# SwiGLU feed-forward on one core: half of the first x rows transposed by the DMA crossbar instead of TensorE

## The chip, the core and the metric

The kernel runs on one core of a Trainium2 chip. A core has a matrix engine (TensorE, PE in the profile), a vector engine (VectorE, DVE), a scalar engine (ScalarE, ACT), GpSimd (POOL) and a sync engine (SyncE, SP). SP and ACT also issue DMA transfers; each has a queue of its own (q1 is SP's, q10 ACT's in this profile), and both queues feed the core's 16 DMA engines. The metric is the device time of one execution in microseconds (us); lower is better.

## The reference

```python
# x (1, 2048, 640), w_gate and w_up (640, 1536), w_down (1536, 640), all bf16
def reference(x, w_gate, w_up, w_down):
    g = silu(x @ w_gate)
    u = x @ w_up
    return (g * u) @ w_down
```

## The kernel before

With P = 128 the 640 columns of x are KD = 5 slices and the 1536 hidden columns are KF = 12 "f chunks". The 2048 rows are worked in four blocks of 512 rows (`sb`), each of four 128-row chunks.

**Layouts.** TensorE contracts over the partition axis, so the gate and up products need x transposed: `xT` holds it as [128 of d, 5, 2048 rows]. Block 0 is loaded plainly into `x_sb` (`load_x`, L84) and transposed by TensorE against an identity matrix (L183), five 128x128 transposes per chunk into a PSUM tile `pt`, which VectorE or ScalarE copies into `xT` (L188). Blocks 1 to 3 come transposed straight from memory by the DMA crossbar (`turn_x`, L125, one DMA of 512 rows each on SP's queue).

**A block.** For each f chunk, `proj` (L192) makes five matmuls for the gate (`pg`) and five for the up product (`pu`), each 128 weights columns by 512 rows of x. ScalarE applies Silu (`sg`, L212) and VectorE multiplies with `pu` into `aT` (L213). PSUM has four buffers for `pg` and `pu` together. After twelve f chunks come the products with `w_down`: `po_t` (columns 512 to 639, transposed) and `po_a` (columns 0 to 511, per 128 rows), their copies and the output DMAs (L276, L301). The last four rows of x are worked on VectorE instead: `row_dots` multiplies transposed weights (`wgT`, `wuT`, loaded through the crossbar by `turn_w`, L129) with `x_row`, spread through blocks 1 to 3.

**The head.** `head()` writes by hand the order in which TensorE works until the third f chunk of block 0, while the loads arrive. 18 filler matmuls on a tile of ones (`warm`, L174) come first; then the transposes of chunks 0 and 2, two fillers, the transposes of chunk 1, two fillers. Then the gate product of f chunk 0 for chunks 0 and 2 (one strided operand, `outer_chunks`) and for chunk 1, the up product of f chunk 0 and the gate product of f chunk 1 for the first 384 rows, the transposes of chunk 3, the up product of f chunk 1 for 384 rows, and the four products for the last 128 rows. `keep_order` fixes the order in which each engine issues its instructions as written.

**The loads.** SP: x chunk 0, x chunk 1, parts of the f chunk 0 slices of `w_gate` and `w_up`, the f chunk 1 slice of `w_gate`, x chunk 3, the f chunk 1 slice of `w_up`, then the later weight slices (`W_CHUNKS`: chunks 2 and 3, 4 to 7, 8 to 11; `load_w`, L81), `w_down`, the crossbar load of block 1, `x_row` and the crossbar loads of `wgT`. ACT: x chunk 2 and the other parts of the two f chunk 0 slices (L111), and then a first small Silu (L114) that has its function table loaded. Each DMA takes one of eight hardware semaphores in turn; a DMA whose semaphore is still held by an earlier one waits in the issuing engine for that one to land.

Of the kernel before, what the change touches and what calls it, by code (L numbers as in the profile page):

```python
# [10 lines left out]
def _body(  # L11
# [8 lines left out]
    nc = tc.nc  # L20
    P = nc.NUM_PARTITIONS
    f32 = mybir.dt.float32
    bf16 = mybir.dt.bfloat16
# [3 lines left out]
    B, S0, D = x.shape  # L27
# [5 lines left out]
    KD = D // P  # L33
    KF = F // P
    S_BLK = 512
    NSB = S // S_BLK
    SUB = S_BLK // P
    DA = 512
    Q = 32
    N_WARM, N_GAP = 18, 2  # L40
    T = 4
    WT_STEP = 4
    ROW_J = 0
    W_CHUNKS = [(0, 1), (1, 2), (2, 4), (4, 8), (8, 12)]
    assert D % P == 0 and F % P == 0 and S % S_BLK == 0 and D > DA and SUB == 4

    consts = ctx.enter_context(tc.tile_pool(name="consts", bufs=1))
# [4 lines left out]
    )  # L52

    ident = consts.tile([P, P], bf16)
    x_sb = consts.tile([P, SUB, D], bf16)
    xT = consts.tile([P, KD, S], bf16)
    wg_sb = consts.tile([P, KD, F], bf16)
    wu_sb = consts.tile([P, KD, F], bf16)
# [13 lines left out]
    xt_v = x2.rearrange("s (kd p) -> s kd p", p=P)  # L72
    wg_v = w_gate.rearrange("(kd p) f -> p kd f", p=P)
    wu_v = w_up.rearrange("(kd p) f -> p kd f", p=P)
    wd_v = w_down.rearrange("(kf p) d -> p kf d", p=P)

    def wslice(a, b):
        return slice(a * P, b * P)

    def load_w(eng, dst, src, a, b):  # L80
        eng.dma_start(out=dst[:, :, wslice(a, b)], in_=src[:, :, wslice(a, b)])  # L81

    def load_x(eng, c0, c1):
        eng.dma_start(out=x_sb[:, c0:c1, :], in_=x_v[:, c0:c1, :])  # L84
# [18 lines left out]
    silu_first = consts.tile([P, 1], f32)  # L103
    nc.vector.memset(ones[:], 1.0)  # L104

    load_x(nc.sync, 0, 1)
    load_x(nc.scalar, 2, 3)
    load_x(nc.sync, 1, 2)
    for dst, src, k in ((wg_sb, wg_v, 3), (wu_sb, wu_v, 2)):
        for eng, k0, k1 in ((nc.scalar, 0, k), (nc.sync, k, KD)):  # L110
            eng.dma_start(out=dst[:, k0:k1, wslice(0, 1)], in_=src[:, k0:k1, wslice(0, 1)])  # L111
    load_w(nc.sync, wg_sb, wg_v, *W_CHUNKS[1])
    load_x(nc.sync, 3, 4)
    nc.scalar.activation(silu_first[:], ones[:, 0:1], ACT.Silu)  # L114
    load_w(nc.sync, wu_sb, wu_v, *W_CHUNKS[1])
    for a, b in W_CHUNKS[2:]:
        load_w(nc.sync, wg_sb, wg_v, a, b)
        load_w(nc.sync, wu_sb, wu_v, a, b)
# [1 line left out]
    wgt_v = w_gate.rearrange("d (kf p) -> d kf p", p=P)  # L120
    wut_v = w_up.rearrange("d (kf p) -> d kf p", p=P)

    def turn_x(sb):
        s_sl = slice(sb * S_BLK, (sb + 1) * S_BLK)
        nc.sync.dma_start_transpose(out=xT[:, :, s_sl], in_=xt_v[s_sl])  # L125

    def turn_w(dst, src):
        for a in range(0, KF, WT_STEP):
            nc.sync.dma_start_transpose(  # L129
                out=dst[:, a : a + WT_STEP, :], in_=src[:, a : a + WT_STEP, :]  # L130
            )

    turn_x(1)
    nc.sync.dma_start(
        out=x_row[:],
        in_=x2[S - T : S, :].rearrange("t d -> (t d)").partition_broadcast(P),
# [29 lines left out]
    def do_dots(n):  # L166
        for _ in range(n):
            next(dots, None)
# [3 lines left out]
    def warm(n):  # L172
        for _ in range(n):
            nc.tensor.matmul(  # L174
                pw[:, 0:P], lhsT=ones[:], rhs=ones[:], start=True, stop=True
            )

    def transpose_chunk(c, parts):
        c_sl = slice(c * P, (c + 1) * P)
        for copy, tag, k0, k1 in parts:  # L180
            pt = psum.tile([P, k1 - k0, P], bf16, tag=tag, name="pt")
            for kd in range(k0, k1):
                nc.tensor.transpose(  # L183
                    out=pt[:, kd - k0, :],
                    in_=x_sb[:, c, kd * P : (kd + 1) * P],
                    identity=ident[:],
                )
            copy(out=xT[:, k0:k1, c_sl], in_=pt[:])  # L188

    def proj(ps, w_sb, fc, sb, c0, c1, cols=lambda ap: ap):  # L190
        for kd in range(KD):
            nc.tensor.matmul(  # L192
                cols(ps[:, c0:c1]),
                lhsT=w_sb[:, kd, fc * P : (fc + 1) * P],
                rhs=cols(xT[:, kd, sb * S_BLK + c0 : sb * S_BLK + c1]),
                start=(kd == 0),
                stop=(kd == KD - 1),
            )

    def outer_chunks(ap):  # L200
        return ap.rearrange("p (c r) -> p c r", r=P)[:, 0:3:2]

    def gu_tiles():
        pg = psum.tile([P, S_BLK], f32, tag="gu", name="pg", bufs=4)
# [12 lines left out]
    def head():  # L217

        dve, act = nc.vector.tensor_copy, nc.scalar.copy
        split = [(act, "po_a", 0, 2), (dve, "po_b", 2, KD)]
        late = (SUB - 1) * P
        (pg0, pu0), (pg1, pu1) = gu_tiles(), gu_tiles()
        warm(N_WARM)
        transpose_chunk(0, [(dve, "po_a", 0, KD)])
        transpose_chunk(2, [(dve, "po_b", 0, KD)])
        warm(N_GAP)  # L230
        transpose_chunk(1, split)
        warm(N_GAP)
        proj(pg0, wg_sb, 0, 0, 0, late, outer_chunks)
        proj(pg0, wg_sb, 0, 0, P, 2 * P)
        proj(pu0, wu_sb, 0, 0, 0, late)
        proj(pg1, wg_sb, 1, 0, 0, late)
        transpose_chunk(3, split)
        proj(pu1, wu_sb, 1, 0, 0, late)
        for fc, pg, pu in ((0, pg0, pu0), (1, pg1, pu1)):
            proj(pg, wg_sb, fc, 0, late, S_BLK)  # L240
            proj(pu, wu_sb, fc, 0, late, S_BLK)
            gate(pg, pu, 0, fc, S_BLK)
        keep_order(mybir.EngineType.PE)
        keep_order(mybir.EngineType.Activation)

    head()
    for sb in range(NSB):
        n_s = S_BLK if sb < NSB - 1 else S_BLK - T
        for fc in range(KF):
            if sb == 0 and fc < 2:  # L250
                continue
            pg, pu = gu_tiles()
            proj(pg, wg_sb, fc, sb, 0, n_s)
            proj(pu, wu_sb, fc, sb, 0, n_s)
            gate(pg, pu, sb, fc, n_s)
            if sb > 0 and fc < KF - 2:
                do_dots(2)


        n_t = (SUB if sb < NSB - 1 else SUB - 1) * P  # L260
        po_t = psum.tile([P, n_t], f32, tag="po_b", name="po_t")
        for kf in range(KF):
            nc.tensor.matmul(  # L263
                po_t[:],
                lhsT=wd_sb[:, kf, DA:D],
                rhs=aT[:, kf, sb * S_BLK : sb * S_BLK + n_t],
                start=(kf == 0),
                stop=(kf == KF - 1),
            )
        ot_t = outp.tile([P, n_t], bf16, name="ot_t")  # L270
        ot_q = outp.tile([P, n_t], bf16, name="ot_q")
        nc.scalar.copy(ot_t[:], po_t[:])  # L272
        do_dots(3)
        nc.vector.transpose(out=ot_q[:], in_=ot_t[:])  # L274
        for q in range(P // Q):
            nc.scalar.dma_start(  # L276
                out=out2[
                    sb * S_BLK : sb * S_BLK + n_t, DA + q * Q : DA + (q + 1) * Q
                ].rearrange("(i r) c -> r i c", r=Q),
                in_=ot_q[q * Q : (q + 1) * Q, :].rearrange("r (i c) -> r i c", c=Q),  # L280
            )

        for j in range(SUB):
            s0 = sb * S_BLK + j * P
            last = sb == NSB - 1 and j == SUB - 1
            po_a = psum.tile([P, DA], f32, tag="po_a", name="po_a")
            for kf in range(KF):
                nc.tensor.matmul(  # L288
                    po_a[:],
                    lhsT=aT[:, kf, s0 : s0 + P],  # L290
                    rhs=wd_sb[:, kf, 0:DA],
                    start=(kf == 0),
                    stop=(kf == KF - 1),
                )
            ot = outp.tile([P, DA], bf16, name="ot")
            nc.scalar.copy(ot[:], po_a[:])  # L296
            if 0 < j:
                do_dots(3)
            if sb == NSB - 1 and j == ROW_J:
                row_tail()  # L300
            nc.sync.dma_start(out=out2[s0 : s0 + P, 0:DA], in_=ot[:])  # L301
            if last:
                po_b = psum.tile([P, D - DA], f32, tag="po_b", name="po_b")
                for kf in range(KF):
                    nc.tensor.matmul(  # L305
                        po_b[:],
                        lhsT=aT[:, kf, s0 : s0 + P],
                        rhs=wd_sb[:, kf, DA:D],
                        start=(kf == 0),
                        stop=(kf == KF - 1),  # L310
                    )
                ot_b = outp.tile([P, D - DA], bf16, name="ot_b")
                nc.vector.tensor_copy(out=ot_b[:], in_=po_b[:])  # L313
                nc.scalar.dma_start(out=out2[s0 : s0 + P, DA:D], in_=ot_b[:])
        if sb == 0:
            turn_x(2)
            turn_w(wuT, wut_v)
            turn_x(3)
    keep_order(mybir.EngineType.DVE)
    keep_order(mybir.EngineType.SP)  # L320

# [104 lines left out]
```

## Time and profile before

| | before |
|---|---|
| median of 3 runs | 164.2 us (164.04 to 164.47) |
| span of the profiled execution, first to last instruction | 163.0 us |
| time outside that span, median less span | 1.2 us |
| TensorE busy | 159.9 us, 98% of the span |
| VectorE, ScalarE busy | 111.7 us, 42.6 us |
| third f chunk of block 0 starts on TensorE | 9.85 us |

The profile gives no total of its own for the profiled execution beside its span, so the span is set against the median of the runs. The profile counts an engine as busy while one of its instructions runs; TensorE's matmuls overlap, so a group of n matmuls is read from the starts of the records. "Landing" is when a DMA's last part has raised its semaphore. In the DMA issues each row is one form of transfer with its size and the median time from issue to landing.

### The profile page before, as it was taken

Reading aid. Unit: us, or ns where it says so; the run is one execution under the profiler, and the core shown is the slowest. Engines: PE = TensorE matmul, PEld = TensorE weight load, DVE = VectorE, ACT = ScalarE, POOL = GpSimd, SP = SyncE. Lnnn points to the kernel's source line nnn. Section 1 sums busy time; section 2 is a strip of 40 time slices with the busy share of each in tenths; the row PEclk is TensorE's granted clock in tenths of the full one; section 3 lists DMA queues with packets and bytes.
Section 4 is the critical chain, followed back from the end, with each engine's and each line's share of the span. In section 5 each row is a group of like instructions: output and inputs, shape, how many; then the busy total and the mean of one; then the engine's idle time right before and its main releaser. Section 6 shows DMA issues by size and latency. Waiting matters only on the chain.

```text
span 163.0 us, 2109 instructions
## 1 busy us (share of the span) xinstructions
PE 159.9 (98%) x787; PEld 77.1 (47%) x799; DVE 111.7 (69%) x251; ACT 42.6 (26%) x73; POOL 0.6 (0%) x6
## 2 busy tenths in 40 slices
PE   9999999999999999999999999999999999999994
PEld 8764444444444444444444444444444444445442
DVE  2133333399559999979919999979964999993000
ACT  3142222212132222222222322221214222222121
POOL 1000000000000000000000000000000000000000
PEclk9999999999999999999999999999999999999999
DMA  7999999993169995003210000000420000000312
GB/s 206 269 342 354 362 229 250 214 198 61 64 123 153 249 186 131 0 0 33 65 64 0 4 0 2 0 0 0 64 68 32 0 0 0 0 4 0 53 35 72
DMA packets 42585, 15.86 MB, mean 97 GB/s; under 512 B 34512, under 2 KB 42448, under 8 KB 42576
## 3 DMA queue, kind: packets, MB, share of 16 engines
q1 hardware_dynamic: 33680, 14.88, 37.0%
q10 hardware_dynamic: 8896, 0.85, 3.8%
q8 instruction: 6, 0.10, 0.2%
q14 instruction: 3, 0.02, 0.1%
HBM read 7.21 MB, written 2.62 MB: 60 GB/s over the span
## 4 chain that ended last, share of the span: by engine, by line
PE 98%; issue 1%; DVE 0%
PE pg L192 32%; PE pu L192 32%; PE po_a L288 25%; PE po_t L263 6%; PE pw L174 2%; PE pt L183 1%; PE po_b L305 0%; DVE ot_b L313 0%; DVE ones L104 0%
## 5 line engine op out<-in xcount | busy, mean ns | idle before, releaser
L192 PE MATMUL pg<-xT,wg_sb 128*128 128x512 bf16 (+4 forms) x248 | 60.3, 370 | 0.4
L192 PE MATMUL pu<-xT,wu_sb 128*128 128x512 bf16 (+3 forms) x250 | 59.9, 370 | 0.0
L213 DVE TENSOR_TENSOR aT<-sg,pu 128x512 bf16<-128x512 f32 (+1 forms) x48 | 32.7, 682 | 29.3 <-PE pu L192 27.9
L212 ACT ACTIVATE sg<-pg 128x512 f32<-128x512 f32 (+1 forms) x48 | 28.6, 596 | 67.4 <-PE pg L192 62.7
L288 PE MATMUL po_a<-wd_sb,aT 128*128 128x512 bf16 x188 | 41.7, 379 | 0.2
L145 DVE SCALAR_TENSOR_TENSOR prod<-wgT,x_row 128x640 f32<-128x640 bf16 x48 | 39.4, 820 | 1.1
L145 DVE SCALAR_TENSOR_TENSOR prod<-wuT,x_row 128x640 f32<-128x640 bf16 x48 | 39.4, 821 | 1.0
L192 PEld LDWEIGHTS <-wg_sb 128*128 128x128 bf16 x255 | 25.0, 100 | 27.6
L192 PEld LDWEIGHTS <-wu_sb 128*128 128x128 bf16 x250 | 24.1, 98 | 27.4
L288 PEld LDWEIGHTS <-aT 128*128 128x128 bf16 x192 | 18.8, 98 | 22.5
L296 ACT CAST ot<-po_a 128x512 bf16<-128x512 f32 x16 | 9.4, 585 | 32.4 <-PE po_a L288 20.7
L263 PE MATMUL po_t<-aT,wd_sb 128*128 128x512 bf16 (+1 forms) x47 | 10.3, 366 | 0.1
L263 PEld LDWEIGHTS <-wd_sb 128*128 128x128 bf16 x48 | 4.7, 98 | 5.1
L313 DVE CAST ot_b<-po_b 128x128 bf16<-128x128 f32 x1 | 0.3, 290 | 9.9 <-PE po_b L305 9.9
L188 DVE COPY xT<-pt 128x640 bf16<-128x640 bf16 (+1 forms) x4 | 1.7, 423 | 6.4 <-PE pt L183 6.4
L272 ACT CAST ot_t<-po_t 128x512 bf16<-128x512 f32 (+1 forms) x4 | 2.2, 558 | 11.6 <-PE po_t L263 11.6
L145 DVE DVE_READ_ACCUMULATOR prod<-wgT,x_row 128x1 f32 x48 | 3.9, 81 | 0.0
L145 DVE DVE_READ_ACCUMULATOR prod<-wuT,x_row 128x1 f32 x48 | 3.9, 81 | 0.0
L274 DVE STREAM_TRANSPOSE ot_q<-ot_t 128x512 bf16<-128x512 bf16 (+1 forms) x4 | 2.7, 678 | 1.7 <-ACT ot_t L272 1.7
L174 PE MATMUL pw<-ones 128*128 128x128 bf16 x22 | 2.9, 313 | 0.4 <-DVE ones L104 0.4
L174 PEld LDWEIGHTS <-ones 128*128 128x128 bf16 x22 | 2.4, 148 | 0.4 <-DVE ones L104 0.4
L183 PE MATMUL pt<-ident,x_sb 128*128 128x128 bf16 x20 | 2.4, 289 | 0.0
(15 smaller groups left out, 7.2 us busy)
## 6 DMA issues: line engine op xcount, KB each, us to landing
out_dram<-ot SPq DMA_DIRECT2D x16, 128.0 KB, 1.7
wd_sb<-in_w_down_dram SPq DMA_DIRECT2D x1, 1920.0 KB, 13.1
wg_sb<-in_w_gate_dram SPq DMA_DIRECT2D x2, 640.0 KB, 7.3
wu_sb<-in_w_up_dram SPq DMA_DIRECT2D x2, 640.0 KB, 8.4
x_row<-in_x_dram SPq DMA_DIRECT2D x1, 640.0 KB, 4.7
x_sb<-in_x_dram SPq DMA_DIRECT2D x3, 160.0 KB, 2.9
out_dram<-ot_q ACTq DMA_DIRECT2D x12, 32.0 KB, 2.0
wg_sb<-in_w_gate_dram SPq DMA_DIRECT2D x1, 320.0 KB, 4.9
```

Source lines behind the costliest of these rows:

```text
L145: nc.vector.scalar_tensor_tensor(out=prod[:], in0=wT[:, fc, :], scalar=1.0, in1=x_row[:, t, :], op0=ALU.mult, op1=ALU.mult, accum_out=acc[ ...
L174: nc.tensor.matmul(pw[:, 0:P], lhsT=ones[:], rhs=ones[:], start=True, stop=True)
L183: nc.tensor.transpose(out=pt[:, kd - k0, :], in_=x_sb[:, c, kd * P : (kd + 1) * P], identity=ident[:],)
L188: copy(out=xT[:, k0:k1, c_sl], in_=pt[:])
L192: nc.tensor.matmul(cols(ps[:, c0:c1]), lhsT=w_sb[:, kd, fc * P : (fc + 1) * P], rhs=cols(xT[:, kd, sb * S_BLK + c0 : sb * S_BLK + c1]), st ...
L212: nc.scalar.activation(sg[:, 0:n_s], pg[:, 0:n_s], ACT.Silu)
L213: nc.vector.tensor_tensor(out=aT[:, fc, s0 : s0 + n_s], in0=sg[:, 0:n_s], in1=pu[:, 0:n_s], op=ALU.mult)
L263: nc.tensor.matmul(po_t[:], lhsT=wd_sb[:, kf, DA:D], rhs=aT[:, kf, sb * S_BLK : sb * S_BLK + n_t], start=(kf == 0), stop=(kf == KF - 1),)
L272: nc.scalar.copy(ot_t[:], po_t[:])
L274: nc.vector.transpose(out=ot_q[:], in_=ot_t[:])
L288: nc.tensor.matmul(po_a[:], lhsT=aT[:, kf, s0 : s0 + P], rhs=wd_sb[:, kf, 0:DA], start=(kf == 0), stop=(kf == KF - 1),)
L296: nc.scalar.copy(ot[:], po_a[:])
```

## The change

Chunks 2 and 3 of x (rows 256 to 511) are no longer loaded plainly and transposed by TensorE; one crossbar DMA of 256 rows writes them into `xT`. `x_sb` holds two chunks instead of four. ACT's queue takes x chunk 1. The f chunk 0 slices of the weights are loaded whole, the gate's by SP and the up product's by ACT, and the f chunk 1 slices follow on ACT's queue; SP issues the crossbar load third, ahead of the later weights. In the head, ten transposes, four PSUM copies and two fillers go; the two f chunks are worked first for rows 0 to 255 (the very first gate product chunk by chunk) and then for rows 256 to 511. `turn_x` takes chunks instead of a block; the loads of blocks 1 to 3 are the same.

```diff
+    PE_X = 2
...
-    x_sb = consts.tile([P, SUB, D], bf16)
+    x_sb = consts.tile([P, PE_X, D], bf16)
...
+    def turn_x(c0, c1):
+        s_sl = slice(c0 * P, c1 * P)
+        nc.sync.dma_start_transpose(out=xT[:, :, s_sl], in_=xt_v[s_sl])
+
     load_x(nc.sync, 0, 1)
-    load_x(nc.scalar, 2, 3)
-    load_x(nc.sync, 1, 2)
-    for dst, src, k in ((wg_sb, wg_v, 3), (wu_sb, wu_v, 2)):
-        for eng, k0, k1 in ((nc.scalar, 0, k), (nc.sync, k, KD)):
-            eng.dma_start(out=dst[:, k0:k1, wslice(0, 1)], in_=src[:, k0:k1, wslice(0, 1)])
-    load_w(nc.sync, wg_sb, wg_v, *W_CHUNKS[1])
-    load_x(nc.sync, 3, 4)
+    load_x(nc.scalar, 1, 2)
+    load_w(nc.sync, wg_sb, wg_v, *W_CHUNKS[0])
+    load_w(nc.scalar, wu_sb, wu_v, *W_CHUNKS[0])
+    turn_x(PE_X, SUB)
+    load_w(nc.scalar, wg_sb, wg_v, *W_CHUNKS[1])
+    load_w(nc.scalar, wu_sb, wu_v, *W_CHUNKS[1])
     nc.scalar.activation(silu_first[:], ones[:, 0:1], ACT.Silu)
-    load_w(nc.sync, wu_sb, wu_v, *W_CHUNKS[1])
     for a, b in W_CHUNKS[2:]:
...
-        late = (SUB - 1) * P
+        late = PE_X * P
         (pg0, pu0), (pg1, pu1) = gu_tiles(), gu_tiles()
         warm(N_WARM)
         transpose_chunk(0, [(dve, "po_a", 0, KD)])
-        transpose_chunk(2, [(dve, "po_b", 0, KD)])
-        warm(N_GAP)
         transpose_chunk(1, split)
         warm(N_GAP)
-        proj(pg0, wg_sb, 0, 0, 0, late, outer_chunks)
-        proj(pg0, wg_sb, 0, 0, P, 2 * P)
+        proj(pg0, wg_sb, 0, 0, 0, P)
+        proj(pg0, wg_sb, 0, 0, P, late)
         proj(pu0, wu_sb, 0, 0, 0, late)
         proj(pg1, wg_sb, 1, 0, 0, late)
-        transpose_chunk(3, split)
         proj(pu1, wu_sb, 1, 0, 0, late)
         for fc, pg, pu in ((0, pg0, pu0), (1, pg1, pu1)):
             proj(pg, wg_sb, fc, 0, late, S_BLK)
```

More of the change, by code (lines that the diff above doesn't have):

```diff
@@ L121, in _body @@
     wut_v = w_up.rearrange("d (kf p) -> d kf p", p=P)
-    def turn_x(sb):
-        s_sl = slice(sb * S_BLK, (sb + 1) * S_BLK)
-        nc.sync.dma_start_transpose(out=xT[:, :, s_sl], in_=xt_v[s_sl])
     def turn_w(dst, src):
@@ L131, in turn_w @@
             )
-    turn_x(1)
+    turn_x(1 * SUB, 2 * SUB)
     nc.sync.dma_start(
@@ L188, in transpose_chunk, with proj @@
             copy(out=xT[:, k0:k1, c_sl], in_=pt[:])
-    def proj(ps, w_sb, fc, sb, c0, c1, cols=lambda ap: ap):
+    def proj(ps, w_sb, fc, sb, c0, c1):
         for kd in range(KD):
             nc.tensor.matmul(
-                cols(ps[:, c0:c1]),
+                ps[:, c0:c1],
                 lhsT=w_sb[:, kd, fc * P : (fc + 1) * P],
-                rhs=cols(xT[:, kd, sb * S_BLK + c0 : sb * S_BLK + c1]),
+                rhs=xT[:, kd, sb * S_BLK + c0 : sb * S_BLK + c1],
                 start=(kd == 0),
@@ L198, in proj @@
             )
-    def outer_chunks(ap):
-        return ap.rearrange("p (c r) -> p c r", r=P)[:, 0:3:2]
     def gu_tiles():
@@ L315, in _body @@
         if sb == 0:
-            turn_x(2)
+            turn_x(2 * SUB, 3 * SUB)
             turn_w(wuT, wut_v)
-            turn_x(3)
+            turn_x(3 * SUB, 4 * SUB)
     keep_order(mybir.EngineType.DVE)
```

## The prediction

> **What bounds the kernel now.** I read the page's busy shares and chain, then the waits, timeline and DMA issues of the first 12 us, the only part that the change touches. From the page:
>
> ```profile
> PE 159.9 (98%) x787; PEld 77.1 (47%) x799; DVE 111.7 (69%) x251; ACT 42.6 (26%) x73; POOL 0.6 (0%) x6
> ...
> PE 98%; issue 1%; DVE 0%
> ```
>
> TensorE is the chain from end to end. The waits of 0 to 12 us (us in total, times, longest) name two for it:
>
> ```profile
> PE pw L174 <- DVE ones L104: 0.4, 1, 0.4
> ...
> PEld L183 <- DMA x_sb<-in_x_dram: 0.2, 1, 0.2
> ```
>
> So the time moves only by what TensorE does or waits for before its third f chunk starts at 9.85, the end of the "head". The timeline (start, us, engine, what):
>
> ```profile
> 0.39 2.10 PE L174 MATMUL pw<-ones 128*128 128x128 bf16 x18 [0.39 <-DVE ones L104]
> ...
> 1.58 1.28 ACT L114 ACT_TABLE_LOAD   x1 [1.58 <-issue]
> ...
> 2.43 1.25 PE L183 MATMUL pt<-ident,x_sb 128*128 128x128 bf16 x10
> ...
> 3.19 1.02 DVE L188 COPY xT<-pt 128x640 bf16<-128x640 bf16 x2 [2.86 <-PE pt L183]
> ...
> 4.44 1.73 PE L192 MATMUL pg<-xT,wg_sb 128*128 128x256 bf16 x10
> ...
> 6.00 0.98 PE L192 MATMUL pu<-xT,wu_sb 128*128 128x384 bf16 x5
> ...
> 7.63 0.44 PE L183 MATMUL pt<-ident,x_sb 128*128 128x128 bf16 x5
> ...
> 9.85 1.24 PE L192 MATMUL pg<-xT,wg_sb 128*128 128x512 bf16 x4
> ```
>
> Two paces are to be seen. Ten transposes at 2.43 start 0.107 apart (their records of 0.31 overlap); five at 7.63 start 0.056 apart. Of the single records the one at 5.92 is the last at the slow pace. The page prints a granted clock of 9 tenths or more all along, so the spacing is what shows it. Slow is 0.83 ns per column, fast 0.43 (0.056/128; 0.1625/384 gives 0.42).
>
> The DMA issues (KB each, us from issue to landing):
>
> ```profile
> wg_sb<-in_w_gate_dram SPq DMA_DIRECT2D x1, 320.0 KB, 4.9
> wu_sb<-in_w_up_dram SPq DMA_DIRECT2D x1, 320.0 KB, 5.6
> ...
> xT<-in_x_dram SPq DMA_TRANSPOSE x3, 5.5
> ```
>
> Issued at 4.11 and 4.52, the slices of chunks 2 and 3 land at 9.0 and 10.1; they are used at 9.85 and 10.92: slack 0.85 and 0.8.
>
> **What goes.** Ten transposes and two filler matmuls: five transposes and two fillers at the slow pace ahead of `pg0`, five at the fast pace later (0.28). The products stay 4 x 5 x 512 = 10,240 columns in as many instructions. ScalarE and VectorE lose two copies each, all off the path.
>
> **The start of `pg0`.** x chunk 0 lands at 2.39, chunk 1, now in chunk 2's place on ACT's queue, at 2.80. Transposes run 2.43 to 3.50, two fillers to 3.71; VectorE's copy of chunk 0 ends at 3.68 as now. ACT issues four loads ahead of its table load, not three: 0.5 later, so the table and the first Silu end at 3.6 instead of 3.07 and chunk 1's copy at 4.0. That copy is needed after five matmuls of 0.107, at 4.2 or later: hidden, by 0.2. The gate slice of chunk 0, now whole on SP, is the last thing due. Today its pieces land at 4.09 and 4.17. By the packet records an x load keeps 16 DMA engines busy for 0.50 (128 packets of 62 ns) and a 128-column slice for 0.71 (640 of 17.7 ns), from 0.95 on. Both whole slices would go out at 0.95 + 2 x 0.50 + 2 x 0.71 = 3.4, and land 0.4 to 1.0 after, as the slices now do. Bounds for `pg0`: 3.74, when the copies allow it, and 4.41, when ACT's whole queue of x and slices lands now. I take 4.05, nearest to today's pieces less the one x load that no longer stands before them. TensorE then idles from 3.71 to 4.05.
>
> Until 5.92 that is 1.87/0.83 = 2,250 columns; the other 7,990 take 3.44 at 0.43 ns, so the head ends at 9.36. The same sum on the kernel now (start 4.44, 10,880 columns with chunk 3's transposes) gives 9.83 against 9.85 seen. Gain 0.47; at the bounds 0.63 and 0.29.
>
> One row speaks of the two queues: from 2.9 to 3.4, with both loaded, some 1,100 packets of 256 B went out per us, and from 3.65 to 4.4, SP's alone, some 660. The Trainium skill (DMA: Bandwidth & Descriptors, Rules for kernel authors) says that spreading over issuing engines brings no bandwidth, since all use the same 16 engines. By that rule both slices run at the single-queue pace and `pg0` starts at about 4.8, which makes the gain 0.08; the trace's stretch speaks against it.
>
> **The crossbar load.** 256 rows x 640 as 1,280 packets of 256 B (the 512-row ones have 2,560). SP issues it third, at about 0.9, behind one x load and one slice; the wait list shows nothing ahead of it. While it issues, SP holds back the chunk 2 and 3 weights, today issued at 4.11. The 512-row load takes 2.97 us to issue on an empty queue and 11.48 behind a backlog; a half is 1.5 at least, and should be over by 3.5, so the weights wait in the queue behind the packets, not in the issue. Landing, lower bound: half the packets of the lone load at 45.6 us: first packet 1.3 after issue, 1.6 of packets, 0.8 to land, so 4.6. By work: 0.95 + 1.00 + 4 x 0.71 + 1,280 x 17.7 ns/16 (1.42) = 6.2, plus 1.05 (today's chunk 1 up slice lands 1.05 after the same sum): 7.25. Transposes also start slowly: the lone one moved 973 packets from 47.0 to 48.5 where 1,700 fit, a loss of 0.65, so 7.9. TensorE wants the rows after four half products: `pg0` to 5.12, `pu0` to 6.06, `pg1` to 6.60, `pu1` to 7.14. Chunk 1's up slice, last on ACT's queue, lands between 5.85 (crossbar packets all behind it) and 7.25 (evenly mixed), wanted at 6.60. Either can be late, hardly both: the packets that delay one hasten the other. I take 0.15 to 0.2 lost here, nearest to 7.25 for the rows.
>
> **Weights behind it.** The crossbar load adds 1.42 and two x loads less take 1.0 off: chunk 2's gate slice lands at 9.0 + 0.42 = 9.4, with the slow start 10.1; chunk 3's at 10.5 to 11.2, wanted 1.08 after the first. With the head ending at 9.36 + 0.2 the first value costs nothing, the second up to 0.55. Later loads (four chunks' slices at 11.9 and 13.8 for 14.2 and 15.2, `wd` at 23.0 for 31.4, rows 512 on at 25.3 for 44.5) keep their slack.
>
> Sum: -0.47 + 0.17 = -0.3. The span is 163.0, the median of the times 164.2, 1.2 beside it; I carry the difference over: 163.9. Faster or slower by 0.3% (0.5 us) is about what a measurement of this kernel can tell from no change.
>
> **Rivals.**
> A, the forecast: short stop at `pg0`, up to 0.3 at the rows: 163.6 to 164.2. Chance 0.41 (0.12 of it beyond 0.5 us of gain).
> B, everything lands in cover, `pg0` at 3.74 to 3.9: gain 0.55 to 0.63, 163.6. For it: fewer bytes before the first slice; against it: no slice has landed before 4.09 yet. 0.13.
> C, slower: the crossbar load does not flow beside copies, so the change doesn't hide it. The one place where it met them:
>
> ```profile
> 20.00:22.00 2.00, 1.95 (x10) 0.94 (x10) 0.69 (x1) 0.44 (x2) 0.00 (x0) 1.00 1.59 279
> 22.00:24.00 2.00, 2.00 (x11) 0.91 (x10) 0.69 (x1) 0.51 (x1) 0.00 (x0) 1.00 0.89 190
> ```
>
> (window, length, busy of five engines, clock, DMA share, GB/s.) The rate falls as `wd`'s tail and the transposes overlap: 490 crossbar packets in 2.4 us, and 570 per half us once the copies are gone, a loss of 2.0. Here the rows would land at 9.25 and the head end at 11.5: 165.8. It decides from a landing at about 7.6 (no gain) and 8.1 (slower). Against it: half the packets, and the copies beside it finish soon. 0.28, at 164.5 to 166; 0.23 of it slower.
> D, the slow pace lasts longer, because of the new idle time at 3.71 to 4.05. The pace changed 3.5 us after the last pause (2.28 to 2.43) and 5.5 after the first matmul. If a pause restarts the count, the change comes at 7.55 (4,200 slow columns, 6,040 at 0.43: end 10.15, 164.5) or, by the longer count, 9.6 (165.5). Against it: one switch in one trace does not show what it counts from. The Trainium skill (TensorE: Matmul & The Clock Gate, Part 1) has the full clock come after a busy window of some 3.4 us that runs freely; by that the pause only matters if it spoils the window, and no trace here shows how much idle time that takes. 0.18, 0.10 of it slower.
>
> **How the numbers follow.** Faster 0.12 + 0.13 = 0.25; slower 0.23 + 0.10 = 0.33; the rest, 0.42, within 0.3%. Forecast 163.9, A's own range 163.6 to 164.2. The range 163.5 to 165.4 leaves out the far part of C, some of D's longer count and a little below: 0.2.
>
> **What would show it.** Right: `pg0` starts at 4.0 to 4.2, the fast pace at about 5.9, chunk 2's gate product at 9.4 to 9.7, and a short wait on the `xT` transposes or none. Wrong: transposes landing after 8, a slow pace beyond 6.5, or a wait for chunk 2's weights as the largest; or an idle TensorE anywhere past 12 us, since I move nothing there.

## The result and the profile after

The change made the kernel slower: 165.56 us (165.17 to 166.99, 6 runs) against 164.12 (163.6 to 164.63, 6 runs) of the kernel before, a ratio of 1.0102 with a 95% interval of 1.0073 to 1.013. The profiled execution's own time is 165.21 and its span 163.9, so 1.3 lie outside the span, about as before. The forecast was 163.9, the range 163.5 to 165.4.

The page of the changed kernel:

```profile
PE 160.2 (98%) x787; PEld 76.7 (47%) x787; DVE 111.0 (68%) x249; ACT 42.2 (26%) x72; POOL 0.6 (0%) x6
...
PE 94%; DMA 4%; ACTq 1%; DVE 0%; issue 0%
```

The busy shares say nothing; the chain does. It was 98% TensorE and now has a DMA in it, which the page's next line names as `wu_sb`; its 4% is the 6.4 us for which that load was in flight, not the time lost. The waits of 0 to 16 us (us in total, times, longest) say where:

```profile
PE pg L191 <- DMA wg_sb<-in_w_gate_dram: 1.1, 1, 1.1
...
PE pw L173 <- DVE ones L105: 0.4, 1, 0.4
...
PE pu L191 <- DMA wu_sb<-in_w_up_dram: 0.2, 1, 0.2
```

and the timeline of the head (start, us, engine, what, idle before):

```profile
1.04 0.55 ACTq L82 DMA_DIRECT2D wg_sb<-in_w_gate_dram  x1
1.62 0.73 ACTq L82 DMA_DIRECT2D wu_sb<-in_w_up_dram  x1
...
3.86 1.25 PE L191 MATMUL pg<-xT,wg_sb 128*128 128x128 bf16 x10
...
4.90 1.12 PE L191 MATMUL pu<-xT,wu_sb 128*128 128x256 bf16 x5
...
7.10 0.72 PE L191 MATMUL pg<-xT,wg_sb 128*128 128x256 bf16 x5 [1.08 <-DMA wg_sb<-in_w_gate_dram]
...
8.05 0.72 PE L191 MATMUL pu<-xT,wu_sb 128*128 128x256 bf16 x5 [0.23 <-DMA wu_sb<-in_w_up_dram]
...
8.61 0.71 PE L191 MATMUL pg<-xT,wg_sb 128*128 128x256 bf16 x5
...
10.79 1.24 PE L191 MATMUL pg<-xT,wg_sb 128*128 128x512 bf16 x5
```

The first gate product starts at 3.86 instead of 4.44: that half of the change worked. Then TensorE stands still for 1.1 us until f chunk 1's gate slice is there, and again before the up slice. From 8.05 on it runs without a break through the products of the crossbar rows. The third f chunk starts at 10.79 instead of 9.85, 0.94 later, and the span is 0.9 longer. From there to the end both profiled executions take 153.1 us, so the whole loss that they show lies in the head, and none of it is a wait for the crossbar load. The two medians are 1.4 apart; the other 0.5 is in executions of which there is no trace. The DMA issues (KB each where given, us to landing):

```profile
wu_sb<-in_w_up_dram ACTq DMA_DIRECT2D x2, 160.0 KB, 5.2
...
wg_sb<-in_w_gate_dram ACTq DMA_DIRECT2D x1, 160.0 KB, 6.0
xT<-in_x_dram SPq DMA_TRANSPOSE x1, 6.9
```

(The row of `wu_sb` gives the median of two loads, the f chunk 0 and the f chunk 1 slice.) The same two slices of f chunk 1 in the kernel before:

```profile
wg_sb<-in_w_gate_dram SPq DMA_DIRECT2D x1, 160.0 KB, 3.9
wu_sb<-in_w_up_dram SPq DMA_DIRECT2D x1, 160.0 KB, 3.6
```

f chunk 1's gate slice, issued at 1.04, lands at 7.05; before, issued at 1.89 on SP's queue, it landed at 5.8. The up slice lands at 8.00, before at 6.83. The crossbar rows land at 7.85, and are wanted only at 8.6, because the waits ahead of them have already cost more.

### The profile page after: what moved, and what is told of

Same layout as the page of the kernel before. It is cut to its first block, busy times and chain, and to the rows that moved or that the text cites. A ratio compares the mean times of both kernels' runs of the same rounds, so it can differ in the third digit from the quotient of the medians.

```text
span 163.9 us, 2091 instructions
## 1 busy us (share of the span) xinstructions
PE 160.2 (98%) x787; PEld 76.7 (47%) x787; DVE 111.0 (68%) x249; ACT 42.2 (26%) x72; POOL 0.6 (0%) x6
## 4 chain that ended last, share of the span: by engine, by line
PE 94%; DMA 4%; ACTq 1%; DVE 0%; issue 0%
PE pu L191 31%; PE pg L191 31%; PE po_a L281 25%; PE po_t L256 6%; DMA wu_sb<-in_w_up_dram 4%; ACTq L82 1%; PE po_b L298 0%; ACTq L85 0%; DVE ot_b L306 0%
## 5 line engine op out<-in xcount | busy, mean ns | idle before, releaser
L191 PE MATMUL pg<-xT,wg_sb 128*128 128x512 bf16 (+3 forms) x255 | 60.4, 370 | 1.1 <-DMA wg_sb<-in_w_gate_dram 1.1
L191 PE MATMUL pu<-xT,wu_sb 128*128 128x512 bf16 (+2 forms) x250 | 60.3, 372 | 0.2 <-DMA wu_sb<-in_w_up_dram 0.2
L191 PEld LDWEIGHTS <-wu_sb 128*128 128x128 bf16 x250 | 24.6, 99 | 27.9 <-DMA wu_sb<-in_w_up_dram 0.5
L187 DVE COPY xT<-pt 128x640 bf16<-128x640 bf16 (+1 forms) x2 | 0.8, 425 | 2.9 <-PE pt L182 2.9
```

The costliest lines, as they stand in the source:

```text
L191: nc.tensor.matmul(ps[:, c0:c1], lhsT=w_sb[:, kd, fc * P : (fc + 1) * P], rhs=xT[:, kd, sb * S_BLK + c0 : sb * S_BLK + c1], start=(kd == 0 ...
```

## The experiments

Two theories stood after this. Theory 1: the crossbar packets, mixed with copies, hold up the slices on ACT's queue. Theory 2: the slices are late because they stand last on ACT's queue, whatever SP's queue carries. After the first results the second was split: theory Q keeps it as it is (ACT's queue is slow as such), and theory P says that the 16 engines serve both queues side by side, so that the slices wait for loads on SP's queue that are wanted later. Every ratio is to the kernel before, timed on the same chip.

### No crossbar load

```diff
-    turn_x(PE_X, SUB)
+    nc.gpsimd.memset(xT[:, :, PE_X * P : SUB * P], 0.05)
```

> The changed kernel without the crossbar load of rows 256 to 511: those columns of xT are set to a constant by GpSimd, so the outputs of these rows are not the reference's. Theory 1 (the crossbar packets beside the copies hold up the f chunk 1 slices): without them chunk 1's gate slice lands at about 5.0 instead of 7.05 and its up slice at about 5.7 instead of 8.00, the wait of 1.1 us at the second gate product is gone, and the third f chunk starts at 9.2 to 9.4 instead of 10.79: about 164.12 - 0.55 = 163.6. Theory 2 (the slices are late because they stand last on ACT's queue behind two others, whatever SP's queue carries): the gate slice still lands at 6.3 or later, a wait of 0.4 us or more stays, and the time is 164.4 or more.

Measured: 165.94 us, ratio 1.0128 (1.0083 to 1.0173). Theory 1 fell. Without a single crossbar packet in the head the slices are no earlier:

```profile
wg_sb<-in_w_gate_dram ACTq DMA_DIRECT2D x1, 160.0 KB, 6.5
```

Issued at 1.03, that is 7.6, against 7.05. The extra half microsecond says little, because this execution was late from its first load on (x chunk 0 landed at 2.79 instead of 2.40). The waits of this kernel's TensorE are

```profile
PE pg L191 <- DMA wg_sb<-in_w_gate_dram: 1.1, 1, 1.1
PE pu L191 <- DMA wu_sb<-in_w_up_dram: 0.7, 1, 0.7
```

With the crossbar load gone, SP's queue goes on at once to the 320 KB slices of f chunks 2 and 3, wanted last of all, and the packet records show them in the engines from 3.25 on, beside f chunk 1's slices on ACT's queue.

### Plain pieces in the crossbar load's place

```diff
-    turn_x(PE_X, SUB)
+    for c in range(PE_X, SUB):
+        nc.sync.dma_start(
+            out=xT[:, :, c * P : (c + 1) * P],
+            in_=x_v[:, c, :].rearrange("p (k r) -> p k r", r=P),
+        )
```

> The changed kernel with the crossbar load replaced, at the same place on SP's queue, by two plain loads of the same 320 KB in as many pieces of 256 B into the same columns of xT; they are not transposed, so the outputs of rows 256 to 511 are not the reference's. If the crossbar as such is what costs, the two queues keep their 1,100 packets per us, chunk 1's gate slice lands at 5.6 to 6.0, the waits at the second f chunk are under 0.3 us together and the third f chunk starts at 9.3 to 9.7: 163.6 to 164.0. If mere bytes and pieces cost, the gate slice lands at about 7 again, the third f chunk starts at 10.6 or later and the time is about 165.3.

Measured: 165.13 us, ratio 1.0073 (1.0041 to 1.0105). Between the two: the gate slice lands at 6.26 instead of 7.05, the waits are 0.4 and 0.7, the third f chunk starts at 10.42. The same bytes on the same queue already cost most of it. The medians leave 0.4 us for the crossbar as such, but the intervals of this ratio and the changed kernel's overlap, so that it is not shown that it adds anything.

### f chunk 1's gate slice ahead of the crossbar load

```diff
+    load_w(nc.sync, wg_sb, wg_v, *W_CHUNKS[1])
     turn_x(PE_X, SUB)
-    load_w(nc.scalar, wg_sb, wg_v, *W_CHUNKS[1])
```

> The changed kernel with f chunk 1's gate slice moved from ACT's queue to SP's, ahead of the crossbar load. If the crossbar packets hold up whatever is queued beside them, the gate slice lands at about 5.2 and the 1.1 us wait for it goes, chunk 1's up slice lands at 6 to 7 and the crossbar rows at 8 to 8.5, wanted at about 7.0: the wait moves to them, the third f chunk starts at 10.2 to 10.7, 164.5 to 165.0. If the place on ACT's queue is the whole cost, nothing else becomes late and the third f chunk starts at 9.4 to 9.7: 163.7 to 164.0.

Measured: 163.93 us, ratio 0.9987 (0.9972 to 1.0002); third f chunk at 9.43. One load moved to the other queue takes back 1.6 us. The gate slice lands at 5.48, the up slice, now the second slice on ACT's queue, at 6.36, and the crossbar rows at 7.21, just when they are wanted. So no large wait took the place of the old one; the first expectation was wrong in that, and the second nearer.

### TensorE's transposes back, the new order kept

```diff
-    x_sb = consts.tile([P, PE_X, D], bf16)
+    x_sb = consts.tile([P, SUB, D], bf16)
...
-    turn_x(PE_X, SUB)
+    load_x(nc.sync, PE_X, SUB)
...
         proj(pg1, wg_sb, 1, 0, 0, late)
+        transpose_chunk(2, split)
+        transpose_chunk(3, split)
```

> The crossbar part undone, the rest of the change kept (whole first slices over both queues, 256-row halves): chunks 2 and 3 of x come by one plain load at the same place on SP's queue, and TensorE makes their ten transposes after the second gate product's first half. If the crossbar load is the cause, pg0 still starts at 3.86, chunk 1's gate slice lands by 5.8, the fast pace comes at about 5.5, and with 640 columns more than now at the fast pace the third f chunk starts at 9.5 to 9.9: 163.8 to 164.2, at or below the kernel before. If the new order of the loads is the cause, the gate slice lands at 6.5 or later and the time is 164.7 or more.

Measured: 166.19 us, ratio 1.0115 (1.0086 to 1.0144), not to be told from the changed kernel's 1.0102. The gate slice lands at 7.33. Undoing the crossbar part while keeping the order of the loads gains nothing. The time alone does not decide, since the ten transposes that are back cost TensorE 0.55 us at the fast pace and 1.06 at the slow one; the landing does: without a crossbar load in the head the gate slice is as late as with it, so the order of the loads is enough to make it late. In this execution even f chunk 0's up slice, second on ACT's queue, landed only at 5.84, and the fast pace of TensorE came at 9.1.

### SP's queue held empty

The first experiment, with one copy more on SP's queue, which makes the loads behind it wait until f chunk 1's up slice has landed:

```diff
+    held = consts.tile([P, P], bf16)
+    nc.sync.dma_start(out=held[:], in_=wu_sb[:, KD - 1, P : 2 * P])
     for a, b in W_CHUNKS[2:]:
```

> The first experiment (no crossbar load, rows 256 to 511 of xT constant) with one more thing: before the slices of f chunks 2 and 3, SP issues a small copy that reads f chunk 1's up slice, so that SP's queue carries nothing from the end of the first gate slice until that slice has landed. Theory P (the 16 engines serve both queues side by side, so f chunk 1's slices on ACT's queue wait for loads on SP's queue that are wanted later): with SP's queue empty the gate slice lands at 4.9 to 5.5 instead of 7.6 and the up slice at 5.4 to 6.2 instead of 9.0; no wait at the second gate product; the held-back slices land at 9.5 or later and TensorE waits for those instead. Theory Q (ACT's queue is slow for its third and fourth load as such): the gate slice still lands at 6.5 or later. The time is not the test; it should be 164.2 to 165.5.

Measured: 165.62 us, ratio 1.0087 (1.0058 to 1.0116). The time was not the test. The two slices, at the same place on ACT's queue, issued at the same moment as in the first experiment:

```profile
wu_sb<-in_w_up_dram ACTq DMA_DIRECT2D x2, 160.0 KB, 4.3
...
wg_sb<-in_w_gate_dram ACTq DMA_DIRECT2D x1, 160.0 KB, 4.5
```

The gate slice lands at 5.53 instead of 7.6 and the up slice at 5.94 instead of 8.95, nothing else being changed but what SP's queue carries. Theory P holds and theory Q falls: ACT's queue is not slow as such; the same 16 engines serve both queues, and each load on SP's queue took its share from a slice that was wanted earlier. The held-back slices come too late instead, as expected (a wait of 0.95 at 9.97).

### Both f chunk 1 slices on SP's queue, ahead of the crossbar load

```diff
+    load_w(nc.sync, wg_sb, wg_v, *W_CHUNKS[1])
+    load_w(nc.sync, wu_sb, wu_v, *W_CHUNKS[1])
     turn_x(PE_X, SUB)
-    load_w(nc.scalar, wg_sb, wg_v, *W_CHUNKS[1])
-    load_w(nc.scalar, wu_sb, wu_v, *W_CHUNKS[1])
```

> The changed kernel with both f chunk 1 slices on SP's queue, ahead of the crossbar load; ACT's queue carries x chunk 1 and the first up slice only. Theory P: everything urgent stands in the order of its use; the gate slice lands at 5.0 to 5.5, the up slice at 5.7 to 6.4, the crossbar rows at 7.2 to 7.8, wanted at about 7.1; the third f chunk starts at 9.4 to 9.9 and the time is 163.8 to 164.2, as with the gate slice alone moved. If the crossbar load costs by its own slowness, the rows land at 8.2 or later and the time is 164.6 or more.

Measured: 163.58 us (163.45 to 163.83), ratio 0.9976 (0.9962 to 0.999): faster than both kernels, 2 us below the changed kernel and about 0.5 below the kernel before. TensorE's waits are down to

```profile
PE pw L173 <- DVE ones L105: 0.4, 1, 0.4
PE pg L191 <- DMA wg_sb<-in_w_gate_dram: 0.3, 1, 0.3
```

The gate slice lands at 5.22, the up slice at 5.78 and the crossbar rows, issued at 2.05, at 6.83:

```profile
xT<-in_x_dram SPq DMA_TRANSPOSE x1, 4.8
```

The crossbar load moved back by two slices and landed a microsecond earlier than in the changed kernel. The third f chunk starts at 9.05. All of this is better than was expected (rows at 7.2 to 7.8, third f chunk at 9.4 to 9.9, 163.8 to 164.2).

### The crossbar part alone, in the third experiment's order

```diff
-    x_sb = consts.tile([P, PE_X, D], bf16)
+    x_sb = consts.tile([P, SUB, D], bf16)
...
     load_w(nc.sync, wg_sb, wg_v, *W_CHUNKS[1])
-    turn_x(PE_X, SUB)
+    load_x(nc.sync, PE_X, SUB)
...
+        transpose_chunk(2, split)
+        transpose_chunk(3, split)
```

> The order of loads that was best so far (f chunk 1's gate slice on SP behind the first gate slice), but x chunks 2 and 3 come plainly at the crossbar load's place and TensorE makes their ten transposes. This prices the crossbar part alone. Under theory P the f chunk 1 slices land in time as with the crossbar (gate about 5.5, up about 6.4) and ten transposes at the fast pace cost 0.56 on TensorE, of which 0 to 0.2 fills a wait: 164.3 to 164.6 against 163.9. If the crossbar load is what hurts, this is faster than 163.9.

Measured: 164.83 us, ratio 1.005 (1.0031 to 1.0068), against 0.9987 (0.9972 to 1.0002) with the crossbar. In this order the crossbar is worth 0.9 us, more than the 0.56 of ten transposes. TensorE also wants the plain rows earlier than it wants transposed ones, and waits 0.7 for them (the rest of this line is x chunk 0):

```profile
PE pt L182 <- DMA x_sb<-in_x_dram: 0.9, 2, 0.7
```

The time is 0.2 above the expected range, and the up slice landed at 7.00, not at about 6.4.

### The kernel before, with chunk 3 alone through the crossbar

```diff
-    load_x(nc.sync, 3, 4)
+    s_late = slice((SUB - 1) * P, SUB * P)
+    nc.sync.dma_start_transpose(out=xT[:, :, s_late], in_=x2.rearrange("s (kd p) -> s kd p", p=P)[s_late])
...
-        transpose_chunk(3, split)
```

> The kernel before with one thing changed: x chunk 3 (rows 384 to 511) comes through the crossbar at its place on SP's queue, 640 packets of 256 B, and its five transposes and two copies go. All loads keep their order and queue. Five transposes at the fast pace are 0.28; the rows are wanted at 8.4 and chunk 3 landed at 6.35 as a plain load. If the crossbar load is harmless where the queue order is right: third f chunk at 9.55 and 0.28 off, 163.9. If the crossbar holds up the slices behind it by 0.5 or more, f chunk 1's up slice lands after 7.4 instead of 6.83, a wait at the up product appears and the gain is gone: 164.2 or more.

Measured: 164.06 us, ratio 1.0011 (0.9994 to 1.0027): no change. f chunk 1's up slice, behind the crossbar rows, lands at 7.32, 0.5 later than before. TensorE could have started that product at 7.11 and starts it at 7.37: 0.26 lost, about the 0.28 that the five transposes cost. TensorE's weight loads show the wait:

```profile
PEld L193 <- DMA wu_sb<-in_w_up_dram: 0.8, 2, 0.5
```

That is the second expectation, with a smaller delay. One profile does not settle it: the fast pace came at 4.6 in it and at 5.9 in the profile of before, so that TensorE wanted the slice earlier, and its third f chunk at 9.40 can't be set against 9.85. This execution also lost 0.7 at 39 us, ahead of a product with `w_down`, which no other profile here shows.

### One queue for all

The sixth experiment with x chunk 1 and the first up slice on SP's queue too.

```diff
-    load_x(nc.scalar, 1, 2)
+    load_x(nc.sync, 1, 2)
     load_w(nc.sync, wg_sb, wg_v, *W_CHUNKS[0])
-    load_w(nc.scalar, wu_sb, wu_v, *W_CHUNKS[0])
+    load_w(nc.sync, wu_sb, wu_v, *W_CHUNKS[0])
```

> As the best so far (both f chunk 1 slices ahead of the crossbar load), but x chunk 1 and the first up slice also on SP's queue: one queue carries every load up to the crossbar rows in the order of use, ACT's queue none. If one queue moves as much as two (theory P as it stands: only the order counts), the first gate slice lands at 3.7 to 4.0 instead of 4.18, the rest as before, the third f chunk starts at 8.9 to 9.2 and the time is 163.3 to 163.6. If one queue moves less, or the later issues on SP tell (each 0.4 to 0.5), x chunk 1 lands after 3.0, f chunk 1's slices after 5.5 and 6.2, the crossbar rows after 7.3, and the time is 163.9 or more.

Measured: 164.68 us, ratio 1.0025 (1.0002 to 1.0049): slower than the sixth, and the expectation that only the order counts was wrong. The first gate slice lands at 4.25, no earlier, and the crossbar load is issued at 3.09 instead of 2.05 and lands at 7.61 instead of 6.83:

```profile
PE pg L191 <- DMA xT<-in_x_dram: 0.5, 1, 0.5
```

That fits a second queue being worth the issue time that it saves; the issue time alone was not varied.

### The pause ahead of the first gate product filled

```diff
-    N_WARM, N_GAP = 18, 2
+    N_WARM, N_GAP = 18, 6
```

> As the best so far, with six filler matmuls instead of two ahead of the first gate product, 0.2 to 0.4 more, which fill TensorE's pause of 0.26 there. If pauses in the first microseconds delay the fast pace, this is faster by 0.1 to 0.4: 163.2 to 163.5. If the pace changes at a time of its own, the pause was free and the fillers cost nothing or up to 0.2: 163.55 to 163.8.

Measured: 163.84 us, ratio 0.9983 (0.9961 to 1.0005), against 0.9976 (0.9962 to 0.999) without: no gain from filling the pause, 0.04 above the range of the second expectation. It does not show that the pause was free, though. In this profile the fast pace came at 4.3 instead of 4.9, and TensorE then stood before the crossbar rows, which landed at 6.96:

```profile
PE pg L191 <- DMA xT<-in_x_dram: 0.3, 1, 0.3
```

With both slices ahead, the landing of these rows sets the time, and an earlier fast pace has nothing to gain.

## Why the prediction was wrong, step by step

**The start of `pg0`**: right in kind, too cautious in size. 3.86 measured, 4.05 taken, 3.74 and 4.41 the bounds. The first gate slice landed at 3.81. Three PSUM copies went, not four (VectorE has 249 instructions for 251, ScalarE 72 for 73); they lie off the path.

**f chunk 1's slices**: the step that failed. The gate slice had no term at all. By the same method (two x loads, three slices, half the crossbar packets: 0.95 + 1.00 + 2.13 + 0.71, plus 1.05) it would have landed at 5.8, ahead of its use at 6.06; it landed at 7.05, for a use at 5.95: 1.1 us. For the up slice I gave 5.85 to 7.25 and it came at 8.00. The method added up packets and divided by 16 engines, as if engine time were dealt out in the order of use. It is dealt out between the two queues. From 4.25 to 5.5 the packet records of the changed kernel show 64 to 85 packets of ACT's queue in each 0.25 us, beside 121 to 173 of SP's; the slices wanted first got a third. And a slice is there only when the last of 16 engines has landed its part: the first engine was done with the gate slice at 5.67, the last at 7.05.

**"Either can be late, hardly both: the packets that delay one hasten the other."** That is where I argued the danger away. The crossbar rows did gain from the share, and it was of no use, because they are wanted after the slices.

**The crossbar load**: 7.25 to 7.9 forecast, 7.85 measured. That it was hidden is luck: TensorE came for the rows only at 8.6, because it had waited for the slices, and by the forecast's own times it would have come at 7.14. Rival C, that it does not flow beside copies, was not what happened: the slices are as late without it (first experiment). It set the right sign with the wrong mechanism.

**Weights behind it**: 9.4 to 10.1 forecast for the gate slice of f chunks 2 and 3, 8.94 measured; 10.5 to 11.2 for their up slice (the prediction speaks of chunk 2's and chunk 3's slices, but each load holds both chunks), 10.0 measured. No wait there, as the sum had it.

**The two queues.** I held against the rule of the Trainium skill (DMA: Bandwidth & Descriptors, Rules for kernel authors) that a second issuing engine brings no bandwidth, only issue time, by a stretch of 660 packets per us on SP's queue alone. With ACT's queue alone in the engines the fifth experiment moved 448, 453 and 407 packets in three half microseconds from 3.5 on, about 870 per us, and the changed kernel's two queues together 447, 334 and 428, about 800 per us, in the same stretch. (SP's packets in that stretch are the crossbar's.) The rule agrees with the runs on bandwidth, and the ninth fits it on issue time. My stretch was not the limit of one queue: the engines were busy 0.79 of it, against 1.28 (records overlap) where both queues moved 1,100 per us. In the changed kernel SP's queue all but alone moved 277 packets in the quarter microsecond from 2.50, 1,100 per us as well. So the start of `pg0` at 4.8 that I worked out for the rule rested on a wrong pace.

**Rival D**, that the pause at 3.7 restarts the count to the fast pace: fell. The pause was there (3.70 to 3.86), and the pace changed at about 5.7, 1.8 after it, not 3.5.

**The sum.** Start of `pg0` and fewer transposes as forecast or better; against that 1.1 + 0.2 of waits that the sum held at 0.17. The wait list counts from the modelled ends of records. By the starts it is 1.6: with 3.86 and the pace change at 5.74 in it, the sum ends the head at 9.2, and it ended at 10.79. Rivals of the slower side had a third of the chance, but the one that came, the order between two queues, was not among them.

## What to carry to other kernels

A load's place is its place across all queues together: a load on a second queue shares the engines with everything on the first, however late that is wanted. Before moving an urgent load to another queue, list what the first queue will carry meanwhile, and price the load as if it got only its share; put what is wanted first at the head of both queues, and anything wanted later behind it on the same queue. Here the same crossbar load is worth nothing or 0.9 us, according to what stands ahead of it.

## What the runs showed of the hardware

The fast pace of TensorE sets in at no fixed time: the spacing of the matmul records changes at about 5.9 in the profile of before, 5.7 in the changed kernel's, 3.6 with the gate slice ahead, 4.9 with both ahead and 9.1 with TensorE's transposes back. The granted clock of 1.00 that the views print for the first microseconds is no measurement: where a trace holds clock records, they begin only at the change (5.95 before, 3.60 with the gate slice ahead, 9.09 with the transposes back), and the changed kernel's trace holds none. Pauses of 0.1 to 0.5 us shortly ahead of it (up to 4.23 in the kernel with both ahead) did not put it off by a fixed count. The free-running window of the Trainium skill (TensorE: Matmul & The Clock Gate, Part 1) fits the changes 3.2 to 5.6 us after the first matmul, and the late one at 9.1 only if the pauses before it spoiled a window, which was not tested.

The first DMA engines to finish a 160 KB slice and the last can be 1.4 us apart (5.67 and 7.05 for the gate slice in the changed kernel), and 0.6 when the other queue is empty (4.90 and 5.53 in the fifth experiment).
